# Moving the inverse transforms of six token tiles from their own stage into the first down projection of a spectral-filter and GEGLU kernel

## Chip, cores, metric

One core of a Trainium2 chip. The metric is the device time of the whole program in microseconds (us), the median of several executions. A profile is one execution; its span runs from the first to the last instruction and is some 2 us shorter than the device time of the same execution. An execution also has a mean granted clock of TensorE (1.000 is full clock).

## The reference, cut to what matters

```python
x = A_x                                            # [1, 2048, 576] bf16
X = rfft2(layernorm(x)) * (w_r + 1j * w_i)         # over tokens and features
h = x + irfft2(X).astype(bfloat16)
n = layernorm(h)
out = h + (gelu(n @ w_gate) * (n @ w_up)) @ w_down # 576 -> 4608 -> 576
```

Both Fourier transforms are done as matrix products with tables. The 2048 tokens are 16 tiles of 128.

## The kernel before

It runs through these parts, TensorE being the common engine:

1. First transforms and the filter, up to a tensor V, which holds for every token tile `c` six blocks of 128 x 128.
2. The inverse stage: for each of 16 tiles the inverse transform over the features ("I", six matmuls of 289 columns over 3 chunks of the frequency k2), an eviction to SBUF, and the inverse transform over the tokens ("N", four matmuls of 288 columns), then the residual add into `XO`.
3. The second layernorm. Tiles 0 to 3 are normalised and transposed inside the inverse stage, because gate/up cannot start before their transposes are in SBUF.
4. Four token blocks of 512 tokens: 36 gate/up steps, then "down" (8 halves of 36 matmuls).

The lines that the argument touches:

```python
TURN = (8, 10, 12, 14)          # transposes of tiles 0..3 come after these tiles

def st_I(c):                     # 6 matmuls of 289 columns, then eviction to GS (ACT)
    for h in range(2):
        for i in range(3):
            i_mm(c, h, i)
    i_ev(c)

def st_N(c):                     # 4 matmuls of 288 columns, then residual add (DVE)
    ...

def norm(c, eng=DVE):            # (x - mean) * rstd, on DVE or on POOL
    ...
    P.op(eng, lambda v, ...: v.tensor_scalar(HN[:, hs, o0:o1], XO[:, c, x0:x1], TM[:, 1, c:c + 1],
                                             RS2[:, c:c + 1], op0=ALU.subtract, op1=ALU.mult), ...)

def turn_pe(c):                  # 5 matmuls with the identity, then one ACT copy of 640 columns
    ...

st_I01()
for c in range(1, NT):
    if c >= 2:
        st_I(c)
    st_N(c - 1)
    ...
    if c == 6:
        ln2_b(0); ln2_c(0)
        norm(0, DVE); norm(1, POOL)
    if c == 7:
        norm(2, DVE); norm(3, POOL)
    if c in TURN:
        turn_pe(TURN.index(c))
```

Of the kernel before, what the change touches and what calls it, by code (L numbers as in the profile page):

```python
# [18 lines left out]
EPS = 1e-5  # L19

# [10 lines left out]
def build_tables():  # L31
# [28 lines left out]
    T["ITAB"] = np.stack([I.reshape(128, -1), -I.reshape(128, -1)], 1).reshape(128, -1)  # L60
# [72 lines left out]
    for t in range(2):  # L133
        dt_[t, :, :K2] = C[128 * t:128 * t + 128]
        dt_[3 + t, :, :K2] = N[128 * t:128 * t + 128]
    dt_[2, 0:33, :K2] = C[256:289]
    dt_[5, 0:32, :K2] = N[256:288]
    T["DTAB"] = dt_.transpose(1, 0, 2).reshape(128, -1)
    T["EYE"] = np.eye(128)
# [156 lines left out]
def _build(nc, A_x, A_w_r, A_w_i, B_w_gate, B_w_up, B_w_down, out):  # L296
# [12 lines left out]
    WGU = sb.alloc("WGU", [128, 4, 9, FF // 4], BF16)  # L309
    wgu_end = sb.off  # L310
    sb.off = wgu_off + 2 * 9 * (FF // 4) * 2
    WS = sb.alloc("WS", [128, NG, 3, KW], BF16)
    sb.off = wgu_end
    HN = sb.alloc("HN", [128, 4, 640], BF16)
# [35 lines left out]
    sb.off = v_off  # L350
    V = sb.alloc("V", [128, 6, NT, NG, 8], BF16)
    DT = sb.alloc("DT", [128, 6, KW], BF16)
    IT = sb.alloc("IT", [128, 2, NT, 128], BF16)
    ES = sb.alloc("ES", [128, 2, 2 * HK], F32)
    YS = sb.alloc("YS", [128, 2, 2, KW], BF16)
    t1_off = sb.off
# [3 lines left out]
    sb.off = t1_off  # L360
# [58 lines left out]
    P.dma(SP, IT[:, :, :, :].rearrange("p a b c -> p (a b c)"), dram["ITAB"][:, :], "it", w=["IT"])  # L419
    P.dma(SP, IDT[:, :], dram["EYE"][:, :], "eye", w=["IDT"])  # L420
# [226 lines left out]

    VBANKS = {NG - 4: (0, 0, 1), NG - 2: (2, 2, 3), LAST: (0, 1, 4)}

    def st_V(i):  # L650
        g = GORD[i]
        sl = i % 3
        sp_ = 1 if g == 0 else 0
        bs = VBANKS.get(i, (6, 6, 7))
        for c in range(3):
            b, o = bs[c], 256 if c == 1 and bs[0] == bs[1] else 0
            if i == PESUM:
                parts = [(zp, ZS[:, 3 * zp, pl, 128 * c:128 * c + 128], ("Z", 3 * zp, 0)) for zp in range(2) for pl in range(2)]
            else:
                parts = [(zp, ZS[:, sl, zp, 128 * c:128 * c + 128], ("Z", sl, int(c > 0))) for zp in range(2)]  # L660
            for m, (zp, lhs, key) in enumerate(parts):
                P.op(PE, lambda t, b=b, o=o, zp=zp, lhs=lhs, sp_=sp_, m=m, n=len(parts): t.matmul(bank(b, 0, 128, o, o + 256), lhs, VT[:, sp_, zp, :],  # L662
                                                                                                start=(m == 0), stop=(m == n - 1)),
                     r=[key, "Zz", "VT"], w=[("PS", b)])
            if i == LAST:
                src = bank(b, 0, 128, 0, 256).rearrange("p (k n e) -> p k n e", k=2, n=16)
                if c < 2:
                    P.op(DVE, lambda v, g=g, c=c, src=src: v.tensor_copy(V[:, 2 * c:2 * c + 2, :, g, :], src), r=[("PS", b), "Vfree"], w=[("V", g, c)])
                else:
                    P.op(ACT, lambda a, g=g, c=c, src=src: a.activation(V[:, 2 * c:2 * c + 2, :, g, :], src, ACTF.Copy), r=[("PS", b), "Vfree"], w=[("V", g, c)])  # L670
        if i < LAST:
            src = PS[:, bs[0] * 512:bs[0] * 512 + 768].rearrange("p (k n e) -> p k n e", k=6, n=16)
            P.op(ACT, lambda a, g=g, src=src: a.activation(V[:, :, :, g, :], src, ACTF.Copy), r=[("PS", bs[0]), ("PS", bs[2]), "Vfree"], w=[("V", g, c) for c in range(3)])  # L673
# [6 lines left out]
    P.alias(["J0", "J1", "ZD"] + [(n_, c) for n_ in ("ATB", "ATS") for c in range(NT)], ["Vfree"])  # L680
# [19 lines left out]
    st_T(LAST, 0, 0, 128, (0,))  # L700
    st_Z(NG - 2)
    st_T(LAST, 1, 0, 128, (0,))
    st_T(LAST, 0, 128, KW, (1,))
    st_Z(LAST, 0, 128, (0,))
    st_T(LAST, 1, 128, KW, (1,))
    st_Z(LAST, 128, KW, (1,))
# [6 lines left out]
    P.alias(wkeys[0] + wkeys[1] + ["Wz"] + [("Wn", i) for i in range(NG)], [("WG", j, k) for j in (2, 3) for k in range(4)])  # L713
    for j in range(4):
        f0, f1 = 1152 * j, 1152 * j + 1152
        for o, (eng, src) in enumerate(((POOL, B_w_gate), (SP, B_w_up))):
            P.dma(eng, WGU[:, j, 4 * o:4 * o + 4, :], src[0:512, f0:f1].rearrange("(t p) f -> p t f", p=128), f"wgu{o}{j}", w=[("WG", j, o)])
            P.dma(eng, WGU[64 * o:64 * o + 64, j, 8, :], src[512:576, f0:f1], f"wgu{o}{j}", w=[("WG", j, 2 + o)])
    P.alias(["FT", "BT", "VT"], [("HT", 0, i, k) for i in range(4) for k in range(5)])

    P.alias([("T", a, t_, h) for a in range(2) for t_ in range(2) for h in range(2)], [("G", a, h) for a in range(2) for h in range(2)])
# [5 lines left out]
    TURN = (8, 10, 12, 14)  # L727

    def islot(c):
        return (c + sum(c > t for t in TURN)) % 2  # L730

    def i_mm(c, h, i):
        b, kt = 2 * islot(c) + h, 2 * i + h
        P.op(PE, lambda t, b=b, h=h, i=i, kt=kt, c=c: t.matmul(bank(b, 0, 128, 0, K2), V[:, kt, c, :, :], DT[:, 3 * h + i, 0:K2],  # L734
                                                              start=(i == 0), stop=(i == 2)), r=vk[i] + ["DT"], w=[("PS", b)])
# [44 lines left out]

    def ln2_a(q):
        c0, c1 = ((0, 4), (4, 16))[q]
        P.op(DVE, lambda v, c0=c0, c1=c1: v.tensor_scalar(TM[:, 1, c0:c1], SB2[:, 0, c0:c1], 1.0 / D, None, op0=ALU.mult), r=[("S0", c) for c in range(c0, c1)], w=[("MN", q)])
        P.op(DVE, lambda v, c0=c0, c1=c1: v.tensor_tensor(TM[:, 0, c0:c1], TM[:, 1, c0:c1], TM[:, 1, c0:c1], op=ALU.mult), r=[("MN", q)], w=[("M2", q)])
        P.op(DVE, lambda v, c0=c0, c1=c1: v.scalar_tensor_tensor(RS2[:, c0:c1], SB2[:, 1, c0:c1], 1.0 / D, TM[:, 0, c0:c1], op0=ALU.mult, op1=ALU.subtract),
             r=[("M2", q)] + [("S1", c) for c in range(c0, c1)], w=[("V2", q)])

    def ln2_b(q):
        c0, c1 = ((0, 4), (4, 16))[q]
        P.op(ACT, lambda a, c0=c0, c1=c1: a.activation(RS2[:, c0:c1], RS2[:, c0:c1], ACTF.Sqrt, bias=EPT[:, 0:1]), r=[("V2", q), "EPT"], w=[("SD2", q)])  # L790

    def ln2_c(q):
        c0, c1 = ((0, 4), (4, 16))[q]
        P.op(DVE, lambda v, c0=c0, c1=c1: v.reciprocal(RS2[:, c0:c1], RS2[:, c0:c1]), r=[("SD2", q)], w=[("RS2", q)])

    def norm(c, eng=DVE):
        hs = c % 4
        q = min(c // 4, 1)
        for i, (o0, o1, x0, x1) in enumerate(((0, D, 0, D), (D, 640, 512, D))):
            P.op(eng, lambda v, c=c, hs=hs, o0=o0, o1=o1, x0=x0, x1=x1: v.tensor_scalar(HN[:, hs, o0:o1], XO[:, c, x0:x1], TM[:, 1, c:c + 1],  # L800
                                                                                        RS2[:, c:c + 1], op0=ALU.subtract, op1=ALU.mult),
                 r=[("X", c), ("MN", q), ("RS2", q)], w=[("HN", hs, i)])

# [8 lines left out]
    def turn_pe(c):  # L812
        hs = c % 4
        t0, t1 = 128 * c, 128 * c + 128
        b0 = 2 * ((TURN[c] + 1 + c) % 2)
# [8 lines left out]
    for c in range(1, NT):  # L824
# [23 lines left out]
    fdead = vkeys + ["DT", "IT", ("G", 0, 0), ("G", 0, 1), ("G", 1, 0), ("G", 1, 1), ("Y", 0), ("Y", 1), "Yz", "Zz"]  # L848
# [107 lines left out]
```

## Time and profile before

Device time 502.35 us (502.28 to 502.42, 3 executions). Read from the profile:

| stretch | us | set by |
|---|---|---|
| first transforms and filter | 0 to 53.45 | DVE for most of it |
| inverse stage, 16 tiles | 53.45 to 74.86 | PE |
| first gate/up | 74.86 to 146.97 | PE |
| first down | 146.97 to 182.36 | PE |
| the rest | 182.36 to 501.0 | PE |

The head of the page of the kernel before (engine, busy us, share of the span, instructions) says that PE has almost no idle time:

```profile
PE 491.8 (98%) x4322; PEld 298.9 (60%) x4323; DVE 182.2 (36%) x390; ACT 158.2 (32%) x296; POOL 39.7 (8%) x49
```

The chain of waits of the kernel before, end of the inverse stage (start us, length us, what it was):

```profile
73.26 0.28 PE PS L818 x5
73.54 0.90 PE PS L734 x6
74.43 0.49 PE PS L773 x4
74.92 1.40 PE PS L872 x6
76.32 0.60 PE PS L773 x4
76.92 70.05 PE PS L872 x648
146.97 35.39 PE PS L895 x288
```

L734 is I and L773 is N: 0.75 us for six matmuls (0.90 straight after a transpose, L818) and 0.49 us for four. L872 is gate/up, L895 is down. Every piece is PE, so every matmul taken out of this stage can come off the time, as long as nothing else then ends later.

In the timeline two norms together fill POOL from 63.04 to 69.31 us. The last transpose comes at 73 us, so nobody waits for them.

```profile
63.04 6.27 POOL L800 TENSOR_SCALAR HN<-XO,TM,RS 128x576 bf16<-128x576 bf16 x4 [7.72 <-DVE RS L794]
```

### The profile page before, as it was taken

How to read it: one execution, taken by the hardware profiler on the slowest of the kernel's cores; microseconds unless marked ns; L12 is line 12 of the kernel's file. 1: busy time of each engine (PE TensorE's matmuls, PEld its weight loads, DVE VectorE, ACT ScalarE, POOL GpSimd, SP SyncE). 2: the span in 40 equal slices, each digit the busy share in tenths (PEclk: the TensorE clock that was granted, in tenths of full speed). 3: DMA queues.
4: the chain of work that ended last, by engine and by line, in shares of the span. 5: the costliest groups of instructions: out<-in, count | busy, mean ns of one | idle time of the engine just before them, and what ended most of it. 6: DMA issues, size and time to landing. Idle time of an engine off the chain costs nothing.

```text
span 501.0 us, 9981 instructions
## 1 busy us (share of the span) xinstructions
PE 491.8 (98%) x4322; PEld 298.9 (60%) x4323; DVE 182.2 (36%) x390; ACT 158.2 (32%) x296; POOL 39.7 (8%) x49
## 2 busy tenths in 40 slices
PE   6899999999999999999999999999999999999998
PEld 2588774444457764444477744444677544444775
DVE  5899663344421114433311034433201233333111
ACT  7888766653220012332300023232100123233000
POOL 3654290000000000000000000000000000000000
DMA  8779889001100000100000001100000000000000
GB/s 283 167 218 350 279 287 316 2 7 25 26 1 19 18 13 20 22 14 1 2 13 12 19 18 21 23 2 1 1 18 19 13 1 1 1 3 1 12 19 19
DMA packets 25948, 28.64 MB, mean 57 GB/s; under 512 B 11568, under 2 KB 19888, under 8 KB 25776
## 3 DMA queue, kind: packets, MB, share of 16 engines
q1 hardware_dynamic: 23328, 17.39, 12.1%
q0 software_dynamic: 2576, 10.62, 6.2%
q8 instruction: 34, 0.56, 0.5%
q14 instruction: 10, 0.08, 0.1%
HBM read 23.66 MB, written 2.36 MB: 52 GB/s over the span
## 4 chain that ended last, share of the span: by engine, by line
PE 90%; DVE 7%; issue 1%; DMA 1%; ACT 0%; SPq 0%; DVEq 0%
PE PS L872 56%; PE PS L895 28%; PE PS L734 3%; DVE TP L639 2%; PE PS L773 2%; DVE ST L440 1%; DVE ZS L644 1%; DMA XO<-in_A_x_dram 1%; DVE CUS L613 1%; PE PS L600 1%; DVE U L505 0%; DVE ATS L472 0%; DVE CUS L610 0%; PE PS L818 0%; DVE MV L449 0%
## 5 line engine op out<-in xcount | busy, mean ns | idle before, releaser
L872 PE MATMUL PS<-HT,WGU 64*128 64x512 bf16 x2592 | 281.9, 377 | 0.0
L872 PEld LDWEIGHTS PS<-HT,WGU 64*128 64x128 bf16 x2592 | 138.1, 94 | 142.6 <-issue 1.2
L884 ACT ACTIVATE GL<-PS 128x512 bf16<-128x512 f32 x144 | 85.9, 597 | 289.3 <-PE PS L872 289.3
L885 DVE TENSOR_TENSOR AT<-GL,PS 128x512 bf16<-128x512 bf16 x144 | 98.9, 687 | 174.2 <-PE PS L872 172.6
L895 PE MATMUL PS<-WD,AT 128*128 128x288 bf16 (+2 forms) x1152 | 141.8, 286 | 0.0
L895 PEld LDWEIGHTS PS<-WD,AT 128*128 128x128 bf16 x1152 | 110.8, 98 | 31.6 <-issue 1.7
L898 DVE TENSOR_TENSOR OS<-PS,XO 128x288 bf16<-128x288 f32 (+2 forms) x32 | 14.6, 458 | 125.8 <-PE PS L895 125.8
L682 POOL TENSOR_SCALAR WS<-WS 128x290 bf16<-128x290 bf16 x16 | 15.7, 982 | 8.9 <-DMA WS<-in_A_w_i_dram 5.1
L776 DVE SCALAR_TENSOR_TENSOR XO<-PS,XO 128x576 bf16<-128x576 f32 x16 | 12.1, 756 | 8.4 <-PE PS L773 8.4
L600 PE MATMUL PS<-FT,U 128*128 128x290 bf16 x96 | 14.4, 287 | 0.5 <-DVE U L505 0.5
L734 PE MATMUL PS<-DT,V 128*128 128x289 bf16 x96 | 14.6, 287 | 0.0
L662 PE MATMUL PS<-VT,ZS 128*128 128x256 bf16 x102 | 13.5, 272 | 0.1
L639 DVE TENSOR_TENSOR TP<-YS,WS 128x580 bf16<-128x580 bf16 (+2 forms) x32 | 13.5, 462 | 0.3 <-issue 0.3
L673 ACT ACTIVATE V<-PS 128x768 bf16<-128x768 f32 x15 | 11.9, 811 | 0.8 <-PE PS L662 0.6
L494 PE MATMUL PS<-ATS,XO 128*128 128x128 bf16 (+1 forms) x80 | 7.1, 223 | 4.6 <-POOL ATS L467 2.7
L632 ACT ACTIVATE YS<-PS 128x578 bf16<-128x578 f32 x16 | 10.5, 654 | 3.5 <-PE PS L629 3.3
L743 ACT ACTIVATE GS<-PS 128x578 bf16<-128x578 f32 x15 | 9.8, 654 | 4.2 <-PE PS L734 4.1
L629 PE MATMUL PS<-CUS,BT 128*128 128x289 bf16 (+2 forms) x96 | 10.7, 247 | 0.3 <-DVE CUS L613 0.3
L600 PEld LDWEIGHTS PS<-FT,U 128*128 128x128 bf16 x96 | 9.2, 98 | 3.0 <-issue 0.7
L734 PEld LDWEIGHTS PS<-DT,V 128*128 128x128 bf16 x96 | 8.9, 97 | 3.4 <-issue 0.3
L764 ACT ACTIVATE OS<-XO 128x576 bf16<-128x576 bf16 x16 | 10.8, 674 | 0.0
L773 PE MATMUL PS<-GS,IT 128*128 128x288 bf16 x64 | 10.5, 285 | 0.0
(59 smaller groups left out, 156.4 us busy)
## 6 DMA issues: line engine op xcount, KB each, us to landing
WD<-in_B_w_down_dram POOLq DMA_DIRECT2D x9, 576.0 KB, 9.1
WGU<-in_B_w_up_dram SPq DMA_DIRECT2D x4, 1152.0 KB, 9.4
WGU<-in_B_w_gate_dram POOLq DMA_DIRECT2D x4, 1152.0 KB, 10.0
out_dram<-OS SPq DMA_DIRECT2D x30, 72.0 KB, 1.6
XO<-in_A_x_dram SPq DMA_DIRECT2D x3, 576.0 KB, 7.4
IT<-c_itab SPq DMA_DIRECT2D x1, 1024.0 KB, 7.1
HT<-HN SPq DMA_TRANSPOSE x60, 2.4
XO<-in_A_x_dram SPq DMA_DIRECT2D x2, 288.0 KB, 3.4
```

The costliest lines, as they stand in the source:

```text
L600: P.op(PE, lambda t, b=b, o=o, dt=dt, us=us, g=g: t.matmul(bank(b, 0, 128, 0, 2 * HK), U[:, us, g, :, :], FT[:, o, dt, :], start=(dt == 0) ...
L639: P.op(DVE, lambda v: v.tensor_tensor(out, YS[:, sl, :, q0:q1], WS[:, g, w_, q0:q1], op=ALU.mult), r=[("Y", sl), ("Wn", i), "Yz", "Zz"] + ...
L662: P.op(PE, lambda t, b=b, o=o, zp=zp, lhs=lhs, sp_=sp_, m=m, n=len(parts): t.matmul(bank(b, 0, 128, o, o + 256), lhs, VT[:, sp_, zp, :], s ...
L682: P.op(POOL, lambda v, g=GORD[i]: v.tensor_scalar(WS[:, g, 0, :], WS[:, g, 2, :], -1.0, None, op0=ALU.mult), r=[k for k in wkeys[0 if 1 <= ...
L734: P.op(PE, lambda t, b=b, h=h, i=i, kt=kt, c=c: t.matmul(bank(b, 0, 128, 0, K2), V[:, kt, c, :, :], DT[:, 3 * h + i, 0:K2], start=(i == 0) ...
L773: P.op(PE, lambda t, b=b, h=h, i=i, c=c, rhs=rhs: t.matmul(bank(b, 0, 128, 0, 288), IT[:, h * i, c, :], rhs, start=(i == 0), stop=(i == 1) ...
L776: P.op(DVE, lambda v, x2=x2, c=c, sl=sl: v.scalar_tensor_tensor(x2, banks(4 + 2 * sl, 2, 288), 1.0, x2, op0=ALU.mult, op1=ALU.add, accum_o ...
L872: op = P.op(PE, lambda t, h0=h0, kt=kt, wt=wt, f=f, b=b, HT=HT, s=(half == 0 and j in (0, 5)), e=(half == 1 and j in (3, 8)): t.matmul(ban ...
L884: P.op(ACT, lambda a, s2=s2, b0=b0: a.activation(GL[:, s2, :], bank(b0), ACTF.Gelu_apprx_tanh), r=[("PS", b0)], w=[("GL", s2)])
L885: P.op(DVE, lambda v, s2=s2, b0=b0, f=f: v.tensor_tensor(AT[:, f, :], GL[:, s2, :], bank(b0 + 1), op=ALU.mult), r=[("GL", s2), ("PS", b0 + ...
L895: P.op(PE, lambda t, b=b, d0=d0, d1=d1, f=f, p=p: t.matmul(bank(b, 0, 128, 0, d1 - d0), AT[:, f, 128 * p:128 * p + 128], WD[:, f, d0:d1], ...
L898: P.op(DVE, lambda v, b=b, d0=d0, d1=d1, p=p, c=c: v.tensor_tensor(OS[:, p % 2, d0:d1], bank(b, 0, 128, 0, d1 - d0), XO[:, c, d0:d1], op=A ...
```

## The change

Tiles 10 to 15 are not needed until the third token block. Their I and N leave the inverse stage and go to the first down projection, one tile ahead of each of its first six halves. There I is folded: even and odd k2 are summed apart (E and O), with half the columns, and the other half of the output follows from E+O and E-O. That is 8 matmuls of 145 columns on PE instead of 6 of 289. DVE then puts the four parts together before N, so N takes 2 matmuls instead of 4. To make room for V to live longer, the four gate/up weight slots become three plus one which shares memory with V; the first slot is loaded twice. The diff, cut to its core:

```diff
+NPRE = 10
-TURN = (8, 10, 12, 14)
+TURN = (8, 9, 9, 9)
-    for c in range(1, NT):
+    for c in range(1, NPRE):
...
+    def def_i(c):                      # even k2 -> bank 2, odd k2 -> bank 3
+        for o in range(2):
+            for t_ in range(2):
+                for i, ch in enumerate((o, 2)):
+                    matmul(bank(2 + o, ..., HK * t_, HK * t_ + HK), V[:, c, 2 * ch + t_], DP[:, 2 * i + o, ...])
+        ACT:  EB = bank 2
+        DVE:  QB[0:2] = EB + bank 3;  QB[2:4] = EB - bank 3
+        DVE:  YB (two operations: halves of the output, one of them reversed)
+    def def_n(c):                      # 2 matmuls of 288, residual add on DVE, square on ACT
     def down(tb, p):
         for h, (d0, d1) in enumerate(((0, cut), (cut, D))):
+            cd = NPRE + 2 * p + h if tb == 0 else NT
+            if cd < NT:
+                def_i(cd)
             for f in range(36):
+                if cd < NT and f == 28:
+                    def_n(cd)
                 matmul(...)            # down
...
+            if tb == 0 and f == 10:
+                wg_load(3, 0)          # slot 0 a second time
+        if tb == 0:
+            ln2_a(2); ln2_b(2); ln2_c(2)
+            wg_load(0, 3)              # the slot that shares memory with V
...
-    TM[:, 1] = SB2[:, 0] * (1.0 / D)        # mean
+    TM[:, 1] = SB2[:, 0] * (-1.0 / D)       # minus the mean
-    norm: op0=ALU.subtract, op1=ALU.mult
+    norm: op0=ALU.add, op1=ALU.mult
...
-    st_T(LAST, 0, 0, 128, (0,))        # last filter group split at column 128
+    st_T(LAST, 0, 0, 256, (0,))        # ... at 256
-    parts: ZS[:, sl, zp, 128 * c:128 * c + 128]
+    parts: ZS[:, sl, zp, ZCOL[c]]      # even columns, odd columns, rest
```

More of the change, by code (lines that the diff above doesn't have):

```diff
@@ L59, in build_tables @@
     T["ATAB"] = A.reshape(128, 16 * 128)
-    T["ITAB"] = np.stack([I.reshape(128, -1), -I.reshape(128, -1)], 1).reshape(128, -1)
+    I = I.reshape(128, 16, 128)
+    T["ITAB"] = np.stack([I[:, :NPRE], -I[:, :NPRE]], 1).reshape(128, -1)
+    T["IDEF"] = I[:, NPRE:].reshape(128, -1)
     k2 = np.arange(HK)[None, :]
@@ L133, in build_tables @@
     for t in range(2):
-        dt_[t, :, :K2] = C[128 * t:128 * t + 128]
-        dt_[3 + t, :, :K2] = N[128 * t:128 * t + 128]
+        dt_[t, :, :K2] = C[t:256:2]
+        dt_[3 + t, :, :K2] = N[t:256:2]
     dt_[2, 0:33, :K2] = C[256:289]
@@ L138, in build_tables @@
     T["DTAB"] = dt_.transpose(1, 0, 2).reshape(128, -1)
+    dp = np.zeros((4, 128, 2, HK))
+    sg = 1 - 2 * (np.arange(K2) % 2 == 0)
+    Ns = N * sg[:, None]
+    for t in range(2):
+        dp[t, :, 0] = C[t:256:2, :HK]
+        dp[t, :, 1] = Ns[t:256:2, :HK]
+        for m in range(33):
+            if m % 2 == t:
+                dp[2 + t, m, 0] = C[256 + m, :HK]
+                dp[2 + t, m, 1] = Ns[256 + m, :HK]
+    T["DPAR"] = dp.transpose(1, 0, 2, 3).reshape(128, -1)
     T["EYE"] = np.eye(128)
@@ L308, in _build @@
     wgu_off = (sb.off + 63) // 64 * 64
-    WGU = sb.alloc("WGU", [128, 4, 9, FF // 4], BF16)
+    slot_bytes = 9 * (FF // 4) * 2
+    WG3 = sb.alloc("WG3", [128, 3, 9, FF // 4], BF16)
     wgu_end = sb.off
-    sb.off = wgu_off + 2 * 9 * (FF // 4) * 2
+    sb.off = wgu_off + slot_bytes
     WS = sb.alloc("WS", [128, NG, 3, KW], BF16)
+    assert sb.off <= wgu_end
     sb.off = wgu_end
+    V = sb.alloc("V", [128, NT, 6, NG, 8], BF16)
+    DP = sb.alloc("DP", [128, 4, 2 * HK], BF16)
+    ITD = sb.alloc("ITD", [128, NT - NPRE, 128], BF16)
+    r3_end = sb.off
+    sb.off = wgu_end
+    WGX = sb.alloc("WGX", [128, 9, FF // 4], BF16)
+    r3_end = max(r3_end, sb.off)
+    sb.off = wgu_end
+    EB = sb.alloc("EB", [128, 2 * HK], F32)
+    QB = sb.alloc("QB", [128, 4, HK + 1], F32)
+    YB = sb.alloc("YB", [128, D], BF16)
+    JD = sb.alloc("JD", [128, D], BF16)
+    assert sb.off <= wgu_end + NPRE * 6 * NG * 8 * 2
+    sb.off = r3_end
     HN = sb.alloc("HN", [128, 4, 640], BF16)
@@ L349, in _build @@
     ZD = sb.alloc("ZD", [128, 512], BF16)
-    sb.off = v_off
-    V = sb.alloc("V", [128, 6, NT, NG, 8], BF16)
     DT = sb.alloc("DT", [128, 6, KW], BF16)
-    IT = sb.alloc("IT", [128, 2, NT, 128], BF16)
+    IT = sb.alloc("IT", [128, 2, NPRE, 128], BF16)
     ES = sb.alloc("ES", [128, 2, 2 * HK], F32)
     YS = sb.alloc("YS", [128, 2, 2, KW], BF16)
-    t1_off = sb.off
     TP = sb.alloc("TP", [128, 2, 2, 2, KW], BF16)
     ZS = sb.alloc("ZS", [128, 4, 2, ZW], BF16)
-    sb.off = t1_off
     GS = sb.alloc("GS", [128, 2, 2, KW], BF16)
@@ L419, in _build @@
     P.dma(SP, IT[:, :, :, :].rearrange("p a b c -> p (a b c)"), dram["ITAB"][:, :], "it", w=["IT"])
+    P.dma(SP, DP[:, :, :].rearrange("p a b -> p (a b)"), dram["DPAR"][:, :], "dp", w=["DP"])
+    P.dma(SP, ITD[:, :, :].rearrange("p a b -> p (a b)"), dram["IDEF"][:, :], "itd", w=["ITD"])
     P.dma(SP, IDT[:, :], dram["EYE"][:, :], "eye", w=["IDT"])
@@ L645, in st_Z @@
              r=[("T", sl, t_, h) for t_ in range(2) for h in hs], w=[("Z", z3, h) for h in hs])
+    ZCOL = (slice(0, 256, 2), slice(1, 256, 2), slice(256, ZW))
     VBANKS = {NG - 4: (0, 0, 1), NG - 2: (2, 2, 3), LAST: (0, 1, 4)}
@@ L657, in st_V @@
             if i == PESUM:
-                parts = [(zp, ZS[:, 3 * zp, pl, 128 * c:128 * c + 128], ("Z", 3 * zp, 0)) for zp in range(2) for pl in range(2)]
+                parts = [(zp, ZS[:, 3 * zp, pl, ZCOL[c]], ("Z", 3 * zp, 0)) for zp in range(2) for pl in range(2)]
             else:
-                parts = [(zp, ZS[:, sl, zp, 128 * c:128 * c + 128], ("Z", sl, int(c > 0))) for zp in range(2)]
+                parts = [(zp, ZS[:, sl, zp, ZCOL[c]], ("Z", sl, int(c > 1))) for zp in range(2)]
             for m, (zp, lhs, key) in enumerate(parts):
@@ L666, in st_V @@
                 src = bank(b, 0, 128, 0, 256).rearrange("p (k n e) -> p k n e", k=2, n=16)
+                dst = V[:, :, 2 * c:2 * c + 2, g, :].rearrange("p n k e -> p k n e")
                 if c < 2:
-                    P.op(DVE, lambda v, g=g, c=c, src=src: v.tensor_copy(V[:, 2 * c:2 * c + 2, :, g, :], src), r=[("PS", b), "Vfree"], w=[("V", g, c)])
+                    P.op(DVE, lambda v, dst=dst, src=src: v.tensor_copy(dst, src), r=[("PS", b)], w=[("V", g, c)])
                 else:
-                    P.op(ACT, lambda a, g=g, c=c, src=src: a.activation(V[:, 2 * c:2 * c + 2, :, g, :], src, ACTF.Copy), r=[("PS", b), "Vfree"], w=[("V", g, c)])
+                    P.op(ACT, lambda a, dst=dst, src=src: a.activation(dst, src, ACTF.Copy), r=[("PS", b)], w=[("V", g, c)])
         if i < LAST:
             src = PS[:, bs[0] * 512:bs[0] * 512 + 768].rearrange("p (k n e) -> p k n e", k=6, n=16)
-            P.op(ACT, lambda a, g=g, src=src: a.activation(V[:, :, :, g, :], src, ACTF.Copy), r=[("PS", bs[0]), ("PS", bs[2]), "Vfree"], w=[("V", g, c) for c in range(3)])
+            dst = V[:, :, :, g, :].rearrange("p n k e -> p k n e")
+            P.op(ACT, lambda a, dst=dst, src=src: a.activation(dst, src, ACTF.Copy), r=[("PS", bs[0]), ("PS", bs[2])], w=[("V", g, c) for c in range(3)])
     def idle_ft(n, b):
@@ L677, in idle_ft @@
             P.op(PE, lambda t, b=b: t.matmul(bank(b, 0, 128, 0, 2 * HK), FT[:, 0, 0, 0:128], FT[:, 0, 0, :], start=True, stop=True), r=["FT"], w=[("PS", b)])
-    P.alias(["J0", "J1", "ZD"] + [(n_, c) for n_ in ("ATB", "ATS") for c in range(NT)], ["Vfree"])
     for i in range(NG):
@@ L699, in _build @@
     st_V(NG - 3)
-    st_T(LAST, 0, 0, 128, (0,))
+    st_T(LAST, 0, 0, 256, (0,))
     st_Z(NG - 2)
-    st_T(LAST, 1, 0, 128, (0,))
-    st_T(LAST, 0, 128, KW, (1,))
-    st_Z(LAST, 0, 128, (0,))
-    st_T(LAST, 1, 128, KW, (1,))
-    st_Z(LAST, 128, KW, (1,))
+    st_T(LAST, 1, 0, 256, (0,))
+    st_T(LAST, 0, 256, KW, (1,))
+    st_Z(LAST, 0, 256, (0,))
+    st_T(LAST, 1, 256, KW, (1,))
+    st_Z(LAST, 256, KW, (1,))
     st_V(NG - 2)
@@ L712, in _build, with wg_tile, wg_load @@
     wdv = B_w_down[:, :].rearrange("(c p) d -> p c d", p=128)
-    P.alias(wkeys[0] + wkeys[1] + ["Wz"] + [("Wn", i) for i in range(NG)], [("WG", j, k) for j in (2, 3) for k in range(4)])
-    for j in range(4):
+    P.alias(wkeys[0] + wkeys[1] + ["Wz"] + [("Wn", i) for i in range(NG)], [("WG", j, k) for j in (1, 2) for k in range(4)])
+    def wg_tile(slot):
+        return WG3[:, slot, :, :] if slot < 3 else WGX[:, :, :]
+    def wg_load(j, slot):
         f0, f1 = 1152 * j, 1152 * j + 1152
+        tile = wg_tile(slot)
         for o, (eng, src) in enumerate(((POOL, B_w_gate), (SP, B_w_up))):
-            P.dma(eng, WGU[:, j, 4 * o:4 * o + 4, :], src[0:512, f0:f1].rearrange("(t p) f -> p t f", p=128), f"wgu{o}{j}", w=[("WG", j, o)])
-            P.dma(eng, WGU[64 * o:64 * o + 64, j, 8, :], src[512:576, f0:f1], f"wgu{o}{j}", w=[("WG", j, 2 + o)])
+            P.dma(eng, tile[:, 4 * o:4 * o + 4, :], src[0:512, f0:f1].rearrange("(t p) f -> p t f", p=128), f"wgu{o}{j}{slot}", w=[("WG", slot, o)])
+            P.dma(eng, tile[64 * o:64 * o + 64, 8, :], src[512:576, f0:f1], f"wgu{o}{j}{slot}", w=[("WG", slot, 2 + o)])
+    for j in range(3):
+        wg_load(j, j)
     P.alias(["FT", "BT", "VT"], [("HT", 0, i, k) for i in range(4) for k in range(5)])
-    P.alias([("T", a, t_, h) for a in range(2) for t_ in range(2) for h in range(2)], [("G", a, h) for a in range(2) for h in range(2)])
     vk = [[("V", g, c) for g in range(NG)] for c in range(3)]
     vkeys = vk[0] + vk[1] + vk[2]
-    TURN = (8, 10, 12, 14)
+    TURN = (8, 9, 9, 9)
+    seq = [("I", 0), ("I", 1)]
+    for c in range(2, NPRE):
+        seq += [("I", c)] + [("T", i) for i in range(4) if TURN[i] == c]
+    seq = {k: i % 2 for i, k in enumerate(seq)}
     def islot(c):
-        return (c + sum(c > t for t in TURN)) % 2
+        return seq["I", c]
     def i_mm(c, h, i):
         b, kt = 2 * islot(c) + h, 2 * i + h
-        P.op(PE, lambda t, b=b, h=h, i=i, kt=kt, c=c: t.matmul(bank(b, 0, 128, 0, K2), V[:, kt, c, :, :], DT[:, 3 * h + i, 0:K2],
+        P.op(PE, lambda t, b=b, h=h, i=i, kt=kt, c=c: t.matmul(bank(b, 0, 128, 0, K2), V[:, c, kt, :, :], DT[:, 3 * h + i, 0:K2],
                                                               start=(i == 0), stop=(i == 2)), r=vk[i] + ["DT"], w=[("PS", b)])
@@ L778, in st_N @@
              r=[("PS", 4 + 2 * sl), ("PS", 5 + 2 * sl)], w=[("X", c), ("S0", c)])
+    QR = ((0, 4), (4, NPRE), (NPRE, NT))
     def ln2_a(q):
-        c0, c1 = ((0, 4), (4, 16))[q]
-        P.op(DVE, lambda v, c0=c0, c1=c1: v.tensor_scalar(TM[:, 1, c0:c1], SB2[:, 0, c0:c1], 1.0 / D, None, op0=ALU.mult), r=[("S0", c) for c in range(c0, c1)], w=[("MN", q)])
+        c0, c1 = QR[q]
+        P.op(DVE, lambda v, c0=c0, c1=c1: v.tensor_scalar(TM[:, 1, c0:c1], SB2[:, 0, c0:c1], -1.0 / D, None, op0=ALU.mult), r=[("S0", c) for c in range(c0, c1)], w=[("MN", q)])
         P.op(DVE, lambda v, c0=c0, c1=c1: v.tensor_tensor(TM[:, 0, c0:c1], TM[:, 1, c0:c1], TM[:, 1, c0:c1], op=ALU.mult), r=[("MN", q)], w=[("M2", q)])
@@ L788, in ln2_b @@
     def ln2_b(q):
-        c0, c1 = ((0, 4), (4, 16))[q]
+        c0, c1 = QR[q]
         P.op(ACT, lambda a, c0=c0, c1=c1: a.activation(RS2[:, c0:c1], RS2[:, c0:c1], ACTF.Sqrt, bias=EPT[:, 0:1]), r=[("V2", q), "EPT"], w=[("SD2", q)])
     def ln2_c(q):
-        c0, c1 = ((0, 4), (4, 16))[q]
+        c0, c1 = QR[q]
         P.op(DVE, lambda v, c0=c0, c1=c1: v.reciprocal(RS2[:, c0:c1], RS2[:, c0:c1]), r=[("SD2", q)], w=[("RS2", q)])
@@ L797, in norm @@
         hs = c % 4
-        q = min(c // 4, 1)
+        q = (c >= 4) + (c >= NPRE)
         for i, (o0, o1, x0, x1) in enumerate(((0, D, 0, D), (D, 640, 512, D))):
             P.op(eng, lambda v, c=c, hs=hs, o0=o0, o1=o1, x0=x0, x1=x1: v.tensor_scalar(HN[:, hs, o0:o1], XO[:, c, x0:x1], TM[:, 1, c:c + 1],
-                                                                                        RS2[:, c:c + 1], op0=ALU.subtract, op1=ALU.mult),
+                                                                                        RS2[:, c:c + 1], op0=ALU.add, op1=ALU.mult),
                  r=[("X", c), ("MN", q), ("RS2", q)], w=[("HN", hs, i)])
@@ L814, in turn_pe @@
         t0, t1 = 128 * c, 128 * c + 128
-        b0 = 2 * ((TURN[c] + 1 + c) % 2)
+        b0 = 2 * seq["T", c]
         for k in range(5):
@@ L839, in _build @@
             norm(3, POOL)
-        if c in TURN:
-            turn_pe(TURN.index(c))
+        for i in range(4):
+            if TURN[i] == c:
+                turn_pe(i)
     P.alias(ukeys + [(n_, a) for n_ in ("CU", "SU") for a in range(3)], [("WD", j) for j in range(9)])
@@ L845, in _build @@
         P.dma(POOL, WD[:, 4 * j:4 * j + 4, :], wdv[:, 4 * j:4 * j + 4, :], f"wd{j}", w=[("WD", j)])
-    fdead = vkeys + ["DT", "IT", ("G", 0, 0), ("G", 0, 1), ("G", 1, 0), ("G", 1, 1), ("Y", 0), ("Y", 1), "Yz", "Zz"]
+    P.alias(vkeys, ["EB", "Q0", "Q1", "YB0", "YB1", "JD"])
+    fdead = ["DT", "IT", "J0", "J1", "ZD"] + [(n_, c) for n_ in ("ATB", "ATS") for c in range(NT)] + [("G", 0, 0), ("G", 0, 1), ("G", 1, 0), ("G", 1, 1), ("Y", 0), ("Y", 1), "Yz", "Zz"]
     fdead += [("T", a, t_, h) for a in range(2) for t_ in range(2) for h in range(2)] + [("E", a) for a in range(2)]
@@ L857, in _build, with fidx @@
     half_done = {}
+    def fidx(m):
+        return m % 36 if m < 36 else (m % 36 + 9) % 36
     def gu(n):
@@ L864, in gu @@
                     continue
-                tb, f = m // 36, m % 36
+                tb, f = m // 36, fidx(m)
+                slot = f // 9 if m < 27 else (3, 1, 2, 0)[f // 9]
                 o, wt = (ASEQ, BSEQ)[half][j]
@@ L871, in gu @@
                 aft = [half_done[m, o]] if half and (j == 0 or j == 4) else []
-                op = P.op(PE, lambda t, h0=h0, kt=kt, wt=wt, f=f, b=b, HT=HT, s=(half == 0 and j in (0, 5)), e=(half == 1 and j in (3, 8)): t.matmul(
-                    bank(b), WGU[h0:h0 + 64, f // 9, wt, 128 * (f % 9):128 * (f % 9) + 128], HT[h0:h0 + 64, kt, :], start=s, stop=e),
-                    r=[("HT", tb % 2, i, k) for i in range(4) for k in range(5)] + [("WG", f // 9, i) for i in range(4)],
+                op = P.op(PE, lambda t, h0=h0, kt=kt, wt=wt, f=f, slot=slot, b=b, HT=HT, s=(half == 0 and j in (0, 5)), e=(half == 1 and j in (3, 8)): t.matmul(
+                    bank(b), wg_tile(slot)[h0:h0 + 64, wt, 128 * (f % 9):128 * (f % 9) + 128], HT[h0:h0 + 64, kt, :], start=s, stop=e),
+                    r=[("HT", tb % 2, i, k) for i in range(4) for k in range(5)] + [("WG", slot, i) for i in range(4)],
                     w=[("PS", b)], after=aft)
@@ L879, in gu @@
         if m < 0:
-            st_N(NT - 1)
+            st_N(NPRE - 1)
             P.alias(fdead, fnew)
             return
-        s2, b0, f = m % 2, 2 * (m % 3), m % 36
+        s2, b0, f = m % 2, 2 * (m % 3), fidx(m)
         P.op(ACT, lambda a, s2=s2, b0=b0: a.activation(GL[:, s2, :], bank(b0), ACTF.Gelu_apprx_tanh), r=[("PS", b0)], w=[("GL", s2)])
@@ L886, in gu @@
              r=[("GL", s2), ("PS", b0 + 1)], w=[("AT", f)])
+    def def_i(c):
+        for o in range(2):
+            for t_ in range(2):
+                for i, ch in enumerate((o, 2)):
+                    P.op(PE, lambda t, o=o, t_=t_, i=i, ch=ch, c=c: t.matmul(bank(2 + o, 0, 128, HK * t_, HK * t_ + HK), V[:, c, 2 * ch + t_, :, :],
+                                                                            DP[:, 2 * i + o, HK * t_:HK * t_ + HK], start=(i == 0), stop=(i == 1)),
+                         r=vk[ch] + ["DP"], w=[("PS", 2 + o)])
+        P.op(ACT, lambda a: a.activation(EB[:, :], bank(2, 0, 128, 0, 2 * HK), ACTF.Copy), r=[("PS", 2)], w=["EB"])
+        e2 = EB[:, :].rearrange("p (a b) -> p a b", a=2)
+        o2 = bank(3, 0, 128, 0, 2 * HK).rearrange("p (a b) -> p a b", a=2)
+        for i, op in enumerate((ALU.add, ALU.subtract)):
+            P.op(DVE, lambda v, i=i, op=op: v.tensor_tensor(QB[:, 2 * i:2 * i + 2, 0:HK], e2, o2, op=op), r=["EB", ("PS", 3)], w=[f"Q{i}"])
+        y2 = YB[:, :].rearrange("p (a b) -> p a b", a=2)
+        P.op(DVE, lambda v: v.tensor_tensor(y2[:, :, 287:143:-1], QB[:, 2::-2, 1:HK], QB[:, 1::2, 1:HK], op=ALU.add), r=["Q0", "Q1"], w=["YB0"])
+        P.op(DVE, lambda v: v.tensor_tensor(y2[:, ::-1, 0:HK - 1], QB[:, 2::-2, 0:HK - 1], QB[:, 1::2, 0:HK - 1], op=ALU.subtract), r=["Q0", "Q1"], w=["YB1"])
+    def def_n(c):
+        for h in range(2):
+            P.op(PE, lambda t, h=h, c=c: t.matmul(bank(4 + h, 0, 128, 0, 288), ITD[:, c - NPRE, :], YB[:, 288 * h:288 * h + 288], start=True, stop=True),
+                 r=["YB0", "YB1", "ITD"], w=[("PS", 4 + h)])
+        x2 = XO[:, c, 0:D].rearrange("p (a b) -> p a b", a=2)
+        P.op(DVE, lambda v, x2=x2, c=c: v.scalar_tensor_tensor(x2, banks(4, 2, 288), 1.0, x2, op0=ALU.mult, op1=ALU.add, accum_out=SB2[:, 0, c:c + 1]),
+             r=[("PS", 4), ("PS", 5)], w=[("X", c), ("S0", c)])
+        square(c, JD[:, :], "JD")
     def down(tb, p):
@@ L892, in down @@
         for h, (d0, d1) in enumerate(((0, cut), (cut, D))):
-            b = (6, 7, 2, 3)[2 * (p % 2) + h]
+            b = (6, 7, 2, 3)[2 * (p % 2) * (tb > 0) + h]
+            cd = NPRE + 2 * p + h if tb == 0 else NT
+            if cd < NT:
+                def_i(cd)
             for f in range(36):
+                if cd < NT and f == 28:
+                    def_n(cd)
                 P.op(PE, lambda t, b=b, d0=d0, d1=d1, f=f, p=p: t.matmul(bank(b, 0, 128, 0, d1 - d0), AT[:, f, 128 * p:128 * p + 128],
@@ L906, in _build @@
             gu(36 * tb + f + 1)
-            if tb == 0 and f < 12:
+            if tb == 0 and f == 10:
+                wg_load(3, 0)
+            if tb == 0 and f < NPRE - 4:
                 square(4 + f, OS[:, f % 2, :], ("OS", f % 2, 0))
@@ L918, in _build @@
             down(tb, p)
+        if tb == 0:
+            ln2_a(2)
+            ln2_b(2)
+            ln2_c(2)
+            P.alias(vkeys + ["DP", "ITD", "EB", "Q0", "Q1", "YB0", "YB1", "JD"], [("WG", 3, k) for k in range(4)])
+            wg_load(0, 3)
     P.op(SP, None, r=[("OUT", i, h) for i in range(2) for h in range(2)])
```

## The prediction

> **What bounds it now.** TensorE: the page shows PE busy 491.8 of 501.0 us (98%); the chain of waits is PE from 52.8 us on. The table of windows has the granted clock at 1.00 everywhere. Spectral filter to 53.45 us (DVE chain), inverse stage 53.45 to 74.86, then four blocks of 70.05 us (gate/up) and 35.39 us (down). In the inverse stage each of 16 tiles costs PE 0.75 us (6 matmuls of 289 columns) plus 0.49 us (4 of 288), 1.24 us.
>
> **What it removes.** Six tiles leave that stage: 6 x 1.24 = 7.4 us, all on the chain.
>
> **What it adds.** In the first down block each of these tiles costs 8 matmuls of 145 columns and 2 of 288. The filter's matmuls of 289+145+144 columns, twice, take 0.51 us for 1156 columns (timeline), so the 8 short ones (1160 columns) take about 0.51 us, and the two long 0.245 us: 0.755 us a tile, 4.5 us in all. The Trainium skill ("TensorE: Matmul & The Clock Gate", Back-to-back issue gap) gives N/2.4 + 2.5 ns, 63 ns at 145, but 81 ns at 128 columns with weight loads; this trace has 128-column transposes at 56 ns (0.28 us for 5), so weight loads should hide. Ideal net: -2.9 us.
>
> **What eats it.** The transposes of the first four normalised tiles were spread to tile 14; now three stand together after tile 9. Two of the norms run on POOL: the timeline has both from 63.04 to 69.31 us, and nothing before them moves. TensorE reaches the last transpose at about 66.9 us and waits for POOL until about 69.25. Then transpose 0.28, latency, ACT eviction 0.70: gate/up can start at about 70.5 us instead of 74.86. So the inverse stage gives back about 4.3 us, not 7.4. Net: -4.3 + 4.5 = about 0.
>
> **Other terms.** The last filter group, split at 256 instead of 128, frees V's second chunk earlier: -0.1 to -0.2 us. Stride-2 weight loads cost nothing extra (98 ns in the first transform, 97 contiguous). In down, ACT copy 0.41 plus four DVE operations at about 0.45, with waits, are done some 3.1 us after a half begins; the token matmul comes at 3.9 us, so no stall, with 0.8 us of margin. An extra Sqrt with two table loads (1.28 us each) falls where ACT is idle.ights: slots 1 and 2 load from 52.4 us on as slots 2 and 3 did (10 us each), needed at about 90; later loads have over 20 us. Small PE bubbles in down: +0.2 us.
>
> **Prediction: 502.4 us**, 80% range 500.9 to 503.9. Faster by over 2%: 0.01; within 2%: 0.98; slower by over 2%: 0.01.
>
> **What would show it.** Right: gate/up starts at 70 to 71 us; a PE wait of 2 to 2.5 us before the last transpose, put down to the POOL norm; the first down block at about 39.9 us instead of 35.4; the others unchanged at 70.05 and 35.39. Wrong if that block is over 40.5 us (late DVE chain, or weight loads bound the short matmuls), or if gate/up starts at about 68.5 (POOL faster without DVE beside it).
>
> **What would make it wrong.** From 66.9 to 70.5 us PE works 0.28 us; the same page (Why this matters) warns of half clock after idle gaps over about 3 us: perhaps +1.5 us. POOL's norm may quicken once DVE falls idle (its two ran 2.52 and 2.28 us): -0.3 us.

(In "Other terms" the record itself is damaged: "ights:" is what is left of the start of a sentence about the weights.)

## More of the kernel before

The groups of instructions by line and shape, POOL alone, of the kernel before (line, engine, operation, output<-inputs, shape, count | busy us, mean ns | idle before): the norm of a tile on POOL.

```profile
L800 POOL TENSOR_SCALAR HN<-XO,TM,RS 128x576 bf16<-128x576 bf16 x2 | 4.8, 2402 | 7.8 <-DVE RS L794 7.7
L800 POOL TENSOR_SCALAR HN<-XO,TM,RS 128x64 bf16<-128x64 bf16 x2 | 1.2, 583 | 0.2
```

## The result

The changed kernel: 502.46 us (501.30 to 503.07, 4 executions) against 502.31 us (4 executions). The ratio is 1.0001, 95% interval 0.9986 to 1.0015: the same. Here and below a ratio is the mean time of one kernel's executions over that of the other's in the same rounds, so it is not quite the ratio of the medians quoted. Executions over 1.5% slower than the fastest of the same kernel are left out of the means. The time does not move, but the executions of the changed kernel spread over 1.8 us, where those of the kernel before lie within 0.2.

The stretches again, from the timelines and chains of the two profiled executions:

| stretch | before us | after us | difference |
|---|---|---|---|
| up to the first matmul of the inverse stage | 53.45 | 53.14 | -0.31 |
| inverse stage to the first gate/up matmul | 21.41 | 15.12 | -6.29 |
| first gate/up | 72.11 | 73.73 | +1.62 |
| first down | 35.39 | 39.91 | +4.52 |
| the rest to the end of the span | 318.64 | 318.70 | +0.06 |
| span | 501.0 | 500.6 | -0.4 |

The chain of waits of the changed kernel over the same stretch (L860 is a transpose, L813 N, L862 the ACT eviction of a transpose, L920 gate/up, L940 and L954 the deferred I and N, L973 down):

```profile
65.85 0.29 PE PS L860 x5
66.14 0.02 issue
66.16 1.96 ACT HT L862 x3
68.12 0.14 issue
68.26 1.45 PE PS L920 x6
69.71 0.86 PE PS L813 x4
70.57 71.42 PE PS L920 x648
141.99 0.61 PE PS L940 x8
142.60 3.43 PE PS L973 x28
146.03 0.24 PE PS L954 x2
146.28 0.98 PE PS L973 x8
```

Three things are to be seen. Gate/up starts at 68.26 us, earlier than the 70.5 that was predicted, and what it waits for is ACT, not POOL. The same 648 gate/up matmuls take 71.42 instead of 70.05 us. And the deferred tiles behave as costed: 0.51 us (0.61 the first time) and 0.24 us a tile, with the down matmuls following without a gap.

POOL's norms in the groups of the changed kernel, same shape and count as before:

```profile
L842 POOL TENSOR_SCALAR HN<-XO,TM,RS 128x576 bf16<-128x576 bf16 x2 | 1.9, 969 | 7.8 <-DVE RS L836 7.7
```

2402 ns have become 969. The timeline of PE alone, changed kernel (start, length, engine, line, what, count, in brackets the idle time before and what ended it):

```profile
66.92 0.45 PE L860 MATMUL PS<-IDT,HN 128*128 128x128 bf16 x5 [0.37 <-ACT HT L862]
68.26 1.45 PE L920 MATMUL PS<-HT,WG 64*128 64x512 bf16 x6 [0.89 <-ACT HT L862]
69.64 0.93 PE L813 MATMUL PS<-GS,IT 128*128 128x288 bf16 x4
```

The last transpose waits for a pair of banks to be evicted by ACT, not for POOL, and gate/up then waits for the last eviction. The table of windows of the changed kernel, with the rows 68:69 and 71:72 left out (window, its length, then busy us and count of PE, PEld, DVE, ACT and POOL, then PEclk, DMA share, GB/s):

```profile
66.00:67.00 1.00, 0.63 (x10) 0.36 (x8) 0.65 (x2) 0.88 (x3) 1.00 (x2) 1.00 1.05 396
67.00:68.00 1.00, 0.37 (x5) 0.20 (x5) 0.00 (x0) 1.00 (x2) 1.00 (x3) 1.00 1.12 371
69.00:70.00 1.00, 1.00 (x7) 0.40 (x5) 0.00 (x0) 0.42 (x1) 1.00 (x2) 0.95 1.00 300
70.00:71.00 1.00, 1.00 (x7) 0.26 (x7) 0.39 (x1) 0.00 (x0) 1.00 (x3) 0.50 1.07 373
72.00:73.00 1.00, 1.00 (x6) 0.41 (x5) 0.00 (x0) 0.56 (x2) 0.37 (x1) 0.50 1.05 396
73.00:74.00 1.00, 1.00 (x10) 0.46 (x8) 0.00 (x0) 0.69 (x3) 0.00 (x0) 0.84 0.97 369
74.00:75.00 1.00, 1.00 (x12) 0.51 (x10) 0.69 (x1) 0.10 (x1) 0.00 (x0) 1.00 1.08 410
```

The last but two number is the granted clock: PE runs at half clock for about 3.4 us, after two windows in which it was busy for only 0.63 and 0.37 us. At half clock 3.4 us do the work of 1.7, which is the 1.6 us that the first gate/up lost. The same stretch before had PE busy throughout and 1.00 everywhere; one of its rows:

```profile
74.00:75.00 1.00, 1.00 (x9) 0.59 (x7) 0.10 (x3) 0.81 (x2) 1.00 (x2) 1.00 1.03 346
```

So two errors of the prediction cancelled: gate/up starts 2.2 us earlier than foreseen, and the clock takes back 1.6 us. The experiments test both, and whether the rest of the sum is right.

### The profile page after: what moved, and what is told of

It is laid out like the page before. It is cut to its first block, busy times and chain, and to the rows that moved or that the text cites. A ratio compares the mean times of both kernels' runs of the same rounds, so it can differ in the third digit from the quotient of the medians.

```text
span 500.6 us, 10028 instructions
## 1 busy us (share of the span) xinstructions
PE 490.3 (98%) x4323; PEld 297.6 (59%) x4323; DVE 192.9 (39%) x418; ACT 159.3 (32%) x299; POOL 38.4 (8%) x51
## 4 chain that ended last, share of the span: by engine, by line
PE 90%; DVE 6%; issue 1%; ACT 1%; DMA 1%; DVEq 0%
PE PS L920 57%; PE PS L973 28%; DVE TP L667 2%; PE PS L774 2%; DVE ST L468 1%; PE PS L813 1%; DVE ZS L672 1%; PE PS L628 1%; PE PS L940 1%; DVE CUS L641 1%; PE PS L691 1%; DMA XO<-in_A_x_dram 1%; DVE U L533 0%; ACT HT L862 0%; PE PS L657 0%
## 5 line engine op out<-in xcount | busy, mean ns | idle before, releaser
L920 PE MATMUL PS<-HT,WG 64*128 64x512 bf16 x2106 | 233.7, 378 | 0.9 <-ACT HT L862 0.9
L920 PEld LDWEIGHTS PS<-HT,WG 64*128 64x128 bf16 x2106 | 113.1, 94 | 117.7 <-issue 3.8
L973 PE MATMUL PS<-WD,AT 128*128 128x288 bf16 (+2 forms) x1152 | 143.6, 286 | 0.0
L973 PEld LDWEIGHTS PS<-WD,AT 128*128 128x128 bf16 x1152 | 110.8, 98 | 30.9 <-issue 1.3
L920 PE MATMUL PS<-HT,WGX 64*128 64x512 bf16 x486 | 56.9, 376 | 0.0
L920 PEld LDWEIGHTS PS<-HT,WGX 64*128 64x128 bf16 x486 | 27.0, 94 | 27.3 <-PE PS L920 0.3
L804 ACT ACTIVATE JD<-XO 128x576 bf16<-128x576 bf16 x6 | 4.1, 684 | 24.8 <-DVE XO L957 24.8
L691 PEld LDWEIGHTS PS<-VT,ZS 128*128 128x128 bf16 x102 | 9.3, 97 | 1.7 <-issue 0.6
L816 DVE SCALAR_TENSOR_TENSOR XO<-PS,XO 128x576 bf16<-128x576 f32 x10 | 7.5, 755 | 6.7 <-PE PS L813 6.7
L468 DVE BATCH_NORM_STATS2 ST<-XO 128x6 f32<-128x288 bf16 x22 | 8.4, 445 | 3.8 <-DMA XO<-in_A_x_dram 3.8
```

The costliest lines, as they stand in the source:

```text
L468: P.op(DVE, lambda v, c=c, h=h: v.bn_stats(ST1[:, c, h, :], XO[:, c, 288 * h:288 * h + 288]), r=[("X", c)], w=[("ST1", c, h)])
L691: P.op(PE, lambda t, b=b, o=o, zp=zp, lhs=lhs, sp_=sp_, m=m, n=len(parts): t.matmul(bank(b, 0, 128, o, o + 256), lhs, VT[:, sp_, zp, :], s ...
L920: op = P.op(PE, lambda t, h0=h0, kt=kt, wt=wt, f=f, slot=slot, b=b, HT=HT, s=(half == 0 and j in (0, 5)), e=(half == 1 and j in (3, 8)): t ...
L973: P.op(PE, lambda t, b=b, d0=d0, d1=d1, f=f, p=p: t.matmul(bank(b, 0, 128, 0, d1 - d0), AT[:, f, 128 * p:128 * p + 128], WD[:, f, d0:d1], ...
```

## Experiments

Theory A: POOL's norm became fast because of its operation, add in place of subtract. Rival B: because of what ran beside it (DVE, DMA, where the tiles lie). Theory C: the half clock comes from too little PE work between the transposes and gate/up. Rival D: it comes from DMA load or from gate/up's own start.

All kernels gave correct results.

### The changed kernel once more

No edit.

> The changed kernel once more, for the spread. If the half-clock window after the transposes comes in every execution, the clock is 0.997 or lower each time and the times lie between 501.3 and 503.1 us, mean near 502.3. If it comes by chance[...], some executions show 1.000 and are some 1.7 us shorter.

Measured: 501.97 us (500.92 to 503.19, 6 executions), ratio to before 0.9991 (0.9978 to 1.0004). Two of the six executions had clock 1.000; they took 501.12 and 500.92 us. The four at 0.997 took 501.56 to 503.19. So it comes by chance, as the second branch had it: an execution can have it or not. (The profile of this run has it, with a first gate/up block of 71.44 us; that of the last run below, "The token matmuls earlier", has not.) An undisturbed execution of the changed kernel takes about 501.0 us, 1.4 us less than the mean of the other four (502.44). The mean clock alone does not decide it: the kernel before also shows 0.997 in more than half of its executions (12 of 20) at no cost (502.0 to 502.7 either way). Presumably such a window falls there where PE waits anyway; no profile of the kernel before caught one. In the profile of the reordered kernel below it stands between 14 and 20 us (granted clock 0.57 and 0.86), among the first transforms, which wait for DVE. So some of the four executions at 0.997, that of 501.56 us above all, may have had theirs there too.

### Subtract put back

```diff
-  TM[:, 1] = SB2[:, 0] * (-1.0 / D);  norm: op0=ALU.add
+  TM[:, 1] = SB2[:, 0] * (1.0 / D);   norm: op0=ALU.subtract
```

> The changed kernel with the normalisation's subtract put back in place of add with a negated mean. Theory A (POOL's subtract is slow, its add fast): the two POOL norms of 576 columns take about 2.3 to 2.5 us again instead of 0.97, the last transpose waits for POOL until about 68.9 us, gate/up starts at about 70.2 us instead of 68.26; the time goes up by about 2 us, to about 504.3. Rival B (POOL ran faster because other engines or DMA beside it had changed): the norms stay at about 1.0 us and the time at 502.4.

Measured: 505.38 us (504.83 to 506.58, 5 executions). Its POOL group, then its last transpose in the timeline of PE:

```profile
L842 POOL TENSOR_SCALAR HN<-XO,TM,RS 128x576 bf16<-128x576 bf16 x2 | 4.8, 2404 | 7.8 <-DVE RS L836 7.7
```

```profile
69.26 0.44 PE L860 MATMUL PS<-IDT,HN 128*128 128x128 bf16 x5 [2.35 <-POOL HN L842]
```

This is A for the norm and for the start of gate/up; the time is 1.1 us above the 504.3 expected. It is also the picture that the prediction drew: a PE wait of 2.35 us before the last transpose, put down to POOL's norm, and gate/up at 70.58 us. A kernel that does fit this picture takes 505.4 us, not the predicted 502.4, and lies outside the stated range of 500.9 to 503.9. The span of the profiled execution is 502.8 against 500.8 of the unedited one, +2.0 us as expected; the medians differ by 3.4. All five executions have a clock of 0.990 to 0.993, that is more time at half clock. In the profiled one this is two windows: one from about 14 to 17 us, which costs nothing to be seen (the inverse stage starts at 53.28 us), and one from about 71.8 to 75 us at the start of gate/up. None of the five escapes as two of the six above did; how the other 1.4 us divide was not taken apart.

### Add in the kernel before

```diff
-  TM[:, 1] = SB2[:, 0] * (1.0 / D);   norm: op0=ALU.subtract
+  TM[:, 1] = SB2[:, 0] * (-1.0 / D);  norm: op0=ALU.add
```

> The kernel before with only the add in place of subtract in the normalisation. Theory A: the two POOL norms fall from 2.40 to about 1.0 us each (576 columns), and since the last transpose comes only at 73 us there, the time stays at 502.3 (within 0.2 us). Rival B: the norms stay at about 2.4 us; time also 502.3.

Measured: 502.20 us (502.13 to 502.74, 5 executions), ratio to before 1.0001 (0.9989 to 1.0013).

```profile
L800 POOL TENSOR_SCALAR HN<-XO,TM,RS 128x576 bf16<-128x576 bf16 x2 | 1.9, 968 | 7.8 <-DVE RS L794 7.7
```

The operation alone does it, with everything else as before. B is out. And in this kernel it is worth nothing, since the norm is not on the chain.

### TensorE kept busy across the two gaps

```diff
     for i in range(4):
         if TURN[i] == c:
             turn_pe(i)
+            if i >= 2:
+                idle_dt((5, 8)[i - 2], 6)   # dummy matmuls of 289 columns into bank 6
```

> The changed kernel with 13 dummy matmuls of 289 columns in the two gaps of TensorE round the last transpose, which fit into its idle time. Theory C (too little PE work before gate/up halves the clock for a window): clock 1.000 in every run, first gate/up block back to about 70.1 us from 71.4, time down by about 1.7 us to about 500.7, or 1 us less of that if the dummies delay something. Rival D (the drop comes from DMA load or from the start of the gate/up matmuls themselves): clock stays at 0.997 and the time at 502.4.

Measured: 501.14 us (500.89 to 501.31, 5 executions), ratio to before 0.9977 (0.9965 to 0.9989). The windows of this kernel:

```profile
69.00:70.00 1.00, 1.00 (x7) 0.36 (x5) 0.00 (x0) 0.53 (x1) 1.00 (x2) 1.00 0.95 302
70.00:71.00 1.00, 1.00 (x10) 0.44 (x10) 0.49 (x1) 0.00 (x0) 1.00 (x3) 1.00 1.07 369
71.00:72.00 1.00, 1.00 (x14) 0.50 (x10) 0.28 (x2) 0.52 (x2) 1.00 (x2) 1.00 0.99 373
```

Its chain of waits:

```profile
70.47 70.05 PE PS L926 x648
```

The clock stays at 1.00 and the block is back at 70.05 us, with the same DMA load and the same gate/up matmuls. One profile alone does not show C, since the changed kernel escapes the half clock at times without dummies too. What shows it is that all five executions lie between 500.89 and 501.31 us, where only four of the ten of the changed kernel lie below 501.6; five in a row by luck would have a chance of about 1% (0.4 to the fifth power, an estimate). That is C. D, that DMA load or gate/up's own start makes the drop by itself, is out on two counts: both are still there here, and they are there in the last run below, at 1.00 without dummies. Thirteen matmuls whose result nobody reads take 0.8 us off the median, and the spread falls from 2.3 us to 0.4. Its level is that of the two undisturbed executions above (about 501.0). Three of the five executions still list a clock of 0.996 or 0.997, at no cost, as in the kernel before; the expectation of 1.000 in every run was wrong in this.

### A better order at the end of the stage

With POOL fast, what holds gate/up back is a row of evictions on ACT (1.96 us of ACT in the chain above). This kernel puts the second transpose ahead of N of tile 8 and N of tile 9 ahead of gate/up, evicts the third transpose on DVE, and gives the fourth its own banks:

```diff
+        if c == NPRE - 1:
+            turn_pe(1)
+            st_N(c - 1, False)      # residual add later
+            turn_pe(2)              # evicted by DVE
+            turn_pe(3)              # banks 6 and 7
+            st_R(c - 1)             # residual add of tile 8
+            st_N(c)                 # banks 2 and 3; was inside gate/up
+            break
```

> The changed kernel with the end of its inverse stage in another order: tile 9's first product, second transpose, tile 8's token matmuls, third and fourth transpose, tile 9's token matmuls, then gate/up. The third transpose is evicted by DVE beside ACT, the fourth uses a third pair of banks, tile 8's residual add on DVE comes after that eviction. If the evictions in a row on ACT were what held gate/up back: gate/up starts at about 67.6 us instead of 68.3 and no longer gives 0.6 us to tile 9's token matmuls; PE idles about 0.6 us instead of 1.8, so the clock should hold. Time about 499.8 us, against 501.0 for executions of the changed kernel at full clock. If the clock still drops: about 501.3.

Measured: 499.90 us (499.47 to 500.03, 5 executions) against 502.15; ratio 0.9953 (0.9939 to 0.9966). It is the fastest version, beating both kernels, though by less than 2%. Its chain of waits and the timeline of PE at the start of gate/up:

```profile
66.92 0.71 ACT HT L874
67.64 0.25 issue
67.88 71.40 PE PS L939 x654
```

```profile
67.88 8.38 PE L939 MATMUL PS<-HT,WG 64*128 64x512 bf16 x70 [0.47 <-ACT HT L874]
```

One eviction is left in the chain instead of three. Gate/up starts at 67.88 us (67.6 expected), no longer makes room for N (71.40 us from there to the down block, against 72.11 before), and the clock is 1.00 from 20 us on. The edit makes several changes at once; which of them is worth how much was not tested.

### Split of the last filter group alone, in the kernel before

```diff
-    st_T(LAST, 0, 0, 128, (0,)) ...
+    st_T(LAST, 0, 0, 256, (0,)) ...
```

> The kernel before with only the last filter group's split at 256 instead of 128 columns. From the first filter matmul to the first matmul of the inverse stage the two profiles of before-like kernels took 32.92 and 32.87 us, the four of changed ones 33.04, 33.06, 33.05 and 32.98. If the split makes this: about 33.04 us. If the new layout of V or the stride-2 weight loads make it: about 32.9 us. The time stays at 502.3 to 502.5.

Measured: 502.18 us (one execution, so its state is unknown; against 502.15), and 32.90 us from the first filter matmul to the first of the inverse stage. It lies with the unsplit ones (32.92 and 32.87). But the two later profiles of changed kernels gave 32.85 and 32.96, inside and outside the group, so differences of 0.1 us cannot be told apart here. What can be said: the gain of 0.1 to 0.2 us that was predicted for the split does not appear.

### The token matmuls earlier in the down half

```diff
-                if cd < NT and f == 28:
+                if cd < NT and f == 12:
```

> The changed kernel with the deferred tile's token matmuls at the 12th matmul of the down half instead of the 28th. By the trace the ACT and DVE chain ends about 2.6 us after the half begins; TensorE would reach the token matmuls at about 0.5 + 12 x 0.1225 = 2.0 us. So it should stall about 0.7 us in each of the 6 halves: first down block about 43.5 to 44.5 us instead of 39.9, time about 506. If the chain is hidden differently from what I read, the block stays at 39.9 us.

Measured: 504.94 us (one execution, state unknown). The timeline shows the token matmuls waiting for the last DVE operation; first the changed kernel's DVE chain in the first half, then this one's wait:

```profile
144.07 0.45 DVE L950 TENSOR_TENSOR YB<-QB 128x288 bf16<-128x288 f32 x1
145.75 0.22 PEld L954 LDWEIGHTS PS<-YB,ITD 128*128 128x128 bf16 x2
```

```profile
142.97 0.41 PE L954 MATMUL PS<-YB,ITD 128*128 128x288 bf16 x2 [0.59 <-DVE YB L950]
```

The stall is real, 0.5 to 0.6 us of PE idle in each half, and the first down block takes 44.0 us (140.29 to 184.32), as expected. The time is 1 us below the 506 expected: this execution did not lose the half clock's 1.6 us. Up to the down block it is the changed kernel unedited, and its chain and windows there are:

```profile
68.19 1.45 PE PS L920 x6
69.64 0.60 PE PS L813 x4
70.24 70.05 PE PS L920 x648
```

```profile
67.00:68.00 1.00, 0.30 (x5) 0.13 (x3) 0.00 (x0) 1.00 (x2) 1.00 (x3) 1.00 1.10 353
70.00:71.00 1.00, 1.00 (x10) 0.40 (x9) 0.72 (x2) 0.00 (x0) 1.00 (x3) 1.00 1.06 364
```

The gaps are the same and the DMA load is as high, yet the clock stays at 1.00 and the block takes 70.05 us (its 0.997 comes from a window between 11 and 17 us). So the gaps make the drop possible and do not force it; when it comes, the stretch from gate/up's start to the down block takes 73.73 us instead of 72.10. In the changed kernel the chain ends at 144.52 us and the weights of the token matmul are loaded at 145.75, a margin of 1.2 us. So the 28th matmul is late enough, and the chain would bind if it were moved forward by more than about 10 matmuls (an estimate: 1.2 us over 0.1225).

## Why the prediction was right, and where not

- **The time, 502.4 against 502.46, and "same": right.** But it rests on two errors of opposite sign, and that they cancel is luck: the kernel with subtract, which does what the prediction described, takes 505.4 us.
- **Removed, 1.24 us of PE a tile: right.** The tiles that stayed still take 0.75 and 0.49 us.
- **Added, 4.5 us in the first down block: right.** 39.91 - 35.39 = 4.52 us. The Trainium skill ("TensorE: Matmul & The Clock Gate", Back-to-back issue gap) gives the gap as N/2.4 + 2.5 ns, which makes an estimate of 63 ns for 145 columns, and a slower figure for 128 columns with weight loads; the eight take 0.51 us, 64 ns each, so the weight loads hide, as the 128-column transposes had shown.
- **The DVE chain in time for the token matmul: right**, with 1.2 us of margin instead of 0.8.
- **"TensorE reaches the last transpose at about 66.9 us and waits for POOL until about 69.25": wrong.** This is the step that failed. The duration of POOL's norm was taken from the trace of before, though the diff changes its operation from subtract to add; the norm went from 2402 to 969 ns. The wait for POOL came only when subtract was put back (2.35 us). Gate/up started 2.2 us earlier than predicted (68.26 instead of 70.5), held by 1.96 us of ACT evictions. By the prediction's own test, "if gate/up starts at about 68.5", this part of it is wrong, and not for the reason named there: with DVE beside it as before, add alone made the norm fast (968 ns in the kernel before).
- **Half clock: named as a risk of +1.5 us but left out of the sum; it belonged in it.** It cost 1.6 us in the profiled execution; the four executions at clock 0.997 took 1.4 us more on average than the two at 1.000. It came although the gaps were shorter than those of the prediction: about 2.1 us from 66.14 to 68.26, with 0.28 us of transposes between.
- **The filter's split, -0.1 to -0.2 us: wrong**, no gain to be seen. **Small bubbles in down, +0.2: wrong**, none was seen.

Where the expected gain of 2.9 us went: removing six tiles saves 7.4 us of PE work and putting them back costs 4.5. The start of gate/up came only 6.6 us earlier (74.86 to 68.26), since the transposes now stand in a row with their evictions exposed, and the half clock took 1.6. That leaves 6.6 - 1.6 - 4.5 = 0.5 us, and the profiled span fell by 0.4. (The profile of the kernel before is a long one, 501.0 us, where its other executions list spans of 500.2 to 500.9; so the medians do not show even that.) With the clock held about 1 us remains of it (501.1), with the order mended as well about 2.3 us (499.9 against 502.15).

## What to carry to other kernels

When work is taken out of a stage, ask what it used to hide: here the matmuls of six tiles covered the evictions of the transposes and kept TensorE's clock up, and both came to light when they left. Read a diff for changes of the operation itself before taking a duration from the old trace; one changed operation was worth about 2 us here once its instruction had come near the chain. Where the clock drops after a short wait of TensorE, as after the 2.1 us here, try useful matmuls in the gap, or, failing that, dummy ones that fit into it. And a prediction that hits the time is not yet a right one: check the waits that it named.

## What the Trainium skill lacked or had wrong

- "TensorE: Matmul & The Clock Gate" (Why this matters for your kernels) advises against gaps over about 3 us. Here the clock was halved in two of the three profiles with these gaps though PE's two gaps, of 0.37 and 0.89 us by the profile, lay in a stretch of only 2.1 us (66.14 to 68.26 us) with 0.28 us of work in it, followed by six gate/up matmuls on half the rows. In the 4 us from 66 to 70 us PE was busy for 2.75. What the same page says of the window (What's actually happening), that it lasts 3413 ns and runs free of the program, agrees: half clock (0.50) for about 3.4 us, and by chance (at least two of six executions escaped).
- The same page (Back-to-back issue gap) gives about 81 ns a matmul at 128 columns with a weight load each. The transposes here take 56 ns (0.28 us for 5), and 145 columns take 64 ns, with a load each.
- "GPSIMD Engine Reference" (Engine selection) calls one-input elementwise work roughly line-rate, and does not tell operations apart. Here `tensor_scalar` of 128x576 bf16 takes 2402 ns with subtract and multiply and 969 ns with add and multiply, in both kernels (128x64: 583 and 395 ns).
